# h - tanh(h) as one constant times tanh(a h)^2 times tanh(b h), from a copy of the PSUM result, on one Trainium2 core

## The chip, the cores and the metric

The kernel runs on 1 core of a Trainium2 chip. The metric is device microseconds of one launch. Times of several runs are given as their median; a profile shows one execution and has a span, from its first to its last instruction.

## The reference

Two blocks follow one another. The first is a linear attention with a decaying state (4 batches, 8 heads, 768 tokens, head width 48); the second is a dense block with 2048 hidden features on the attention's 3072 x 384 result.

```python
for t in range(S):
    cur = einsum('bhd,bhe->bhde', u[None] * k[t], v[t])
    y[:, :, t] = einsum('bhd,bhde->bhe', r[t], state + cur)
    state = w[t][..., None] * state + einsum('bhd,bhe->bhde', k[t], v[t])
x = y.transpose(0, 2, 1, 3).reshape(3072, 384)
h = x @ w_in              # 384 -> 2048
g = h - np.tanh(h)
out = g @ w_out           # 2048 -> 384
```

With the reference's inputs h is small: its standard deviation is 0.0143 and its largest magnitude 0.084.

## The kernel before

**Tiles.** The 3072 tokens are cut into 8 blocks of 384 (4 batches, two blocks each). A block has 16 steps f, each of which makes one tile of h: 128 features by 384 tokens. So there are 128 tiles, numbered `now = i * 16 + f`. While the dense steps of block i run, the attention of block i + 1 is woven between them.

**One step.** `first` puts three fp32 products (six matrix instructions in the trace) into one PSUM bank, `hp`. ScalarE copies it, scaled, into an SBUF tile `h` (L893). Then `slight` makes g = h - tanh(h) for small h as a polynomial: `s` = h^2, `qa` = (s + SHIFT)^2, then on VectorE h := TOP h s (first `product`) and g = (qa + REST) h (second `product`). TensorE uses g some steps later.

**The guard.** The polynomial holds for h^2 up to `SLIGHT`. For the 113 tiles in `light` ScalarE makes all of `s` (Square, L979), `qa` (Square with a bias, L980) and a Relu with a summed output (L984) that is zero if all h^2 are small. For the other 15 tiles (`plain`: the first 13 of block 0 and the last two of the program) VectorE squares h and keeps the largest (`tensor_tensor_reduce`, L994), and ScalarE makes only `qa` (L997). All guards are counted at the end; if one fails, everything is computed again by a general path (`any_h`).

**Order.** TensorE, VectorE, ScalarE and SyncE run the order in which the code is written (a manual schedule); each executes its queue in order. The VectorE work of a step is a list `ops`, in which the two products of the step before (`rest`) are interleaved with attention work. A step's bank `hp` is single from step 6 on: `first` of the next step cannot start before ScalarE has copied it out. (The first six steps use six places in other banks in turn.) The tiles `h`, `s` and `qa` have three buffers each.

**Block 0** has a second job for ScalarE: the weights arrive as raw 64-bit words and are converted to fp32 by three ScalarE instructions per unit (L267: one to `w_sb`, two to `up`) and one VectorE instruction (L271). There are 16 units; `PIECES` says how many of the ScalarE instructions stand in each step f, and these end in step 12. In block 0, g goes straight into the second product (`Second.add`, L1043), three steps after it was made. In later blocks VectorE forms sums of pieces of g (L1013), so that fewer products are needed (`Fewer`, L1092). In block 7, and in a few steps of blocks 3 to 6 (`JOINED`), two tiles of h are made together (L951, L961), without the copy.

Of the kernel before, what the change touches and what calls it, by code (L numbers as in the profile page):

```python
# [37 lines left out]
F32 = mybir.dt.float32  # L38
# [3 lines left out]
BF16 = mybir.dt.bfloat16  # L42
# [3 lines left out]
AF = mybir.ActivationFunctionType  # L46
ALU = mybir.AluOpType
# [4 lines left out]
P = 128  # L52
L = 64
NB = 384
NQ = S // NB
NCH = NB // L
NCP = NCH // 2
NPAIR = H // 2
LP = L + 1
WIDE = NPAIR * NCH * LP  # L60
HALF = WIDE // 2 + 2
UP = 2
# [6 lines left out]
NF = FF // P  # L69
# [10 lines left out]
LATE = 3  # L80
# [41 lines left out]
JOINED = {3: (1,), 4: (1,), 5: (1,), 6: (1, NF // 2 - 1), 7: TWOS}  # L122


SLIGHT = 2.0 ** -6
TOP, SHIFT, REST = 0.053459249436855316, -1.2470279932022095, 4.680200099945068


@with_exitstack
def kernel(  # L130
# [19 lines left out]
    early = ExitStack()  # L150
    conv = early.enter_context(tc.tile_pool(name="conv", bufs=RAWS))

    shift = const.tile([P, 6], F32, name="shift", tag="shift")
    for i, value in enumerate((QUAD[0][0], QUAD[1][0], -SMALL, -1.0, SHIFT, -SLIGHT)):
        nc.vector.memset(shift[:, i:i + 1], value)
    u_sb = const.tile([P, NPAIR], F32, name="u_sb", tag="u_sb")
    nc.scalar.dma_start(out=u_sb, in_=uT)
# [64 lines left out]
    def ring(t, at, n):  # L222
        return t[:, at + n % 4 * 3:at + n % 4 * 3 + 3].rearrange("p t c -> p (t c)")
# [3 lines left out]
    def g_at(q, x):  # L227
        if not isinstance(x, str):
# [7 lines left out]
    fast = range(1, blocks_n)  # L236
    few = [0 if i not in fast else NF if i + 1 < blocks_n else 2 * LAST for i in range(blocks_n)]
    n_whole = blocks_n * NPAIR * NCH
    light = [n for n in range(blocks_n * NF) if NF - LATE <= n < blocks_n * NF - 2 and
             (n < NF or few[n // NF])]  # L240
    plain = [n for n in range(blocks_n * NF) if n not in light]
    n_excess, n_top = 2 * blocks_n + len(light), len(plain)
    holds = const.tile([P, n_whole + n_excess + n_top], BF16, name="holds", tag="holds")
    ends = const.tile([P, 3], F32, name="ends", tag="ends")
    excess = const.tile([P, n_excess], F32, name="excess", tag="excess")
# [640 lines left out]
    def first(xT, f, hp, apart=0):  # L886
        for kc in reversed(range(KC)):
            nc.tensor.matmul(hp, lhsT=w_in_sb[:, f, kc, :], rhs=xT[kc],  # L888
                             start=(kc == KC - 1), stop=(kc == 0))
            for _ in range(apart):  # L890
                nc.tensor.nop(nofuse=True, hint="apart")
        h = dense.tile([P, NB], F32, name="h", tag="h")
        return h, nc.scalar.activation(out=h, in_=hp, func=AF.Copy, scale=1.0 / UPSCALE)  # L893

    def product(out, in0, scalar, in1, op0):
        return lambda: nc.vector.scalar_tensor_tensor(out=out, in0=in0, scalar=scalar, in1=in1,  # L896
# [67 lines left out]
                               (h[:, 1], h[:, 6], e1[:, 1, 0:HB]),  # L964
                               (h[:, 2:4], twice(h[:, 5]), e1[:, 1::-1, HB:NB]))]

    def slight(h, n, i, f, scale=1.0, later=None):

        s, qa = (dense.tile([P, NB], F32, name=name, tag=name) for name in ("s", "qa"))
        q, j = divmod(f, 2)
        if i in fast:
            g = G[:, g_at(q, "0" + "ab"[j]):g_at(q, "2" + "ab"[j]) + 1].rearrange("p t c -> p (t c)")
        else:
            g = ring(sums, 0, n)
        if n in light:
            at = 2 * blocks_n + light.index(n)
            nc.scalar.activation(out=s, in_=h, func=AF.Square, scale=scale)  # L979
            nc.scalar.activation(out=qa, in_=s, func=AF.Square, bias=shift[:, 4:5])  # L980
            junk = work.tile([P, UP * NCH * LP], BF16, name="junk", tag="junk", bufs=1)

            def over():
                nc.scalar.activation(out=junk[:, 0:NB], in_=s, func=AF.Relu, bias=shift[:, 5:6],  # L984
                                     accum_out=excess[:, at:at + 1])

            if later is None:
                over()
            else:
                later.append(over)  # L990
            square = first = []
        else:
            at = plain.index(n)
            square = [lambda: nc.vector.tensor_tensor_reduce(  # L994
                out=s, in0=h, in1=h, scale=1.0, scalar=0.0, op0=ALU.mult, op1=ALU.max,
                accum_out=top[:, at:at + 1])]
            first = [lambda: nc.scalar.activation(out=qa, in_=s, func=AF.Square, bias=shift[:, 4:5])]  # L997
        return g, first, square, [product(h, h, TOP * scale, s, ALU.mult),
                                  product(g, qa, REST, h, ALU.add)]

    def two(t, a, b):

# [10 lines left out]
        return lambda: nc.vector.tensor_tensor(out=G[:, to:to + 2], in0=two(G, g_at(q, a0), g_at(q, a1)),  # L1013
                                               in1=two(G, g_at(q, b0), g_at(q, b1)), op=OPS[op])

    def any_h(h, g):
        s, qa = (dense.tile([P, NB], F32, name=name, tag=name) for name in ("s", "qa"))
        th, qb, big = (inp.tile([P, 2 * HALF], F32, name=name, tag=tag)[:, 0:NB]
                       for name, tag in (("th", "k"), ("qb", "r"), ("big", "w")))
        nc.scalar.activation(out=s, in_=h, func=AF.Square)  # L1020
        nc.scalar.activation(out=qa, in_=s, func=AF.Square, bias=shift[:, 0:1])
        nc.scalar.activation(out=qb, in_=s, func=AF.Square, bias=shift[:, 1:2])
        nc.scalar.activation(out=th, in_=h, func=AF.Tanh)
        nc.scalar.activation(out=big, in_=s, func=AF.Relu, bias=shift[:, 2:3])
        nc.vector.tensor_tensor(out=th, in0=h, in1=th, op=ALU.subtract)
        product(h, h, SERIES, s, ALU.mult)()
        product(h, qa, QUAD[0][1], h, ALU.add)()
        product(g, qb, QUAD[1][1], h, ALU.add)()
        nc.vector.copy_predicated(out=g, mask=big.bitcast(I32), data=th)
        return g  # L1030
# [284 lines left out]
        pieces = boot(Turns([scratch(ps_boot)] + ps_a.both), [hp] + acc, blocks[0], blocks[1])  # L1315
    ps_d = mains.enter_context(tc.tile_pool(name="ps_d", bufs=1, space=PSUM))
    acc += [ps_d.tile([P, BANK], F32, name=f"acc{j}", tag=f"acc{j}") for j in range(1, NB // P)]
    ahead_of_h, rest, formed, extra, behind, due, summed = [], [], [], [], [], [], []
    held_back, forming, late, carried = [], [], [], []

    def between(ops, others):
# [9 lines left out]

    def sum_held(held, squares, over, to):

        nc.vector.tensor_single_scalar(held, squares, SLIGHT, op=ALU.is_le)
        nc.vector.tensor_reduce(out=to, in_=over, op=ALU.add, axis=mybir.AxisListType.X)

    def form_w(n, q, k):
# [7 lines left out]
    for i, blk in enumerate(blocks):  # L1345
# [8 lines left out]
        second = Second(row0, acc, few[i]) if few[i] < NF else None  # L1354
        for f in range(NF):
            now = i * NF + f
            for op in ahead_of_h if i else ():
                op()
            spare_a, spare_b = (t[:, 0] for t in ps_a.both)
            to = [acc[0], acc[1], hp, spare_a, spare_b, spare_a][now] if now < 6 else hp  # L1360
            joined = f // 2 in JOINED.get(i, ())
            near = later and f < 4
            outs = []
            if not joined:
                h, made = first(here, f, to[:, 0:NB], SPACED[i][f > 12 + (i < 2)])
            elif f % 2 == 0:
                for op in behind:
                    op()
                behind = []
                by = beside if near else twos  # L1370
                outs = by.begin(ps_a, f // 2)
                if near:
                    for name in ("split 2 0", "split 2 1", "split 0 01"):
                        later.phase(ps_a, name)
            if not i:
                made_up = converting(pieces, (PIECES[f] if f < len(PIECES) else 1) - 1)
                for op in ahead_of_h:
                    op()
                made_up += converting(pieces, 1 if f < len(PIECES) and PIECES[f] else 0)
            if not joined:  # L1380
                g, ahead_of_h, square, later_ops = slight(h, now, i, f)
            elif f % 2:
                g, ahead_of_h, square, later_ops = slight(by.h[1], now, i, f, 1.0 / UPSCALE, over)
                for op in over:
                    op()
            else:
                ahead_of_h, square = [], []
            some = ({4: (0, 2), 6: (2, 4), 8: (4, 6), 9: (6, 8), 14: (8, len(SUMS))} if after else
                    {4: (0, 2), 6: (2, 4), 8: (4, 6), 9: (6, 8), 11: (8, 10), 12: (10, len(SUMS))} if later else
                    {4: (0, 1), 5: (1, 2), 6: (2, 3), 7: (3, 4), 8: (4, 5), 9: (5, 9), 10: (9, 11),  # L1390
# [77 lines left out]
                op()  # L1468
            if outs:
                add_due(now)  # L1470
                over = []
                g, ahead_of_h, square, later_ops = slight(by.h[0], now, i, f, 1.0 / UPSCALE, over)
            rest, behind, formed, forming, held_back = later_ops, [], [], held_back, []
            extra = [] if i else made_up
            if f < few[i]:
# [60 lines left out]
                later.together(ps_a)  # L1536
        if fewer and later:
            summed.append(fewer)
    nc.vector.tensor_single_scalar(ends[:, 1:3], top[:, n_top - 2:], SLIGHT, op=ALU.is_le)
    again = const.tile([1, 1], I32, name="again", tag="again")  # L1540
    for op in ahead_of_h + rest:
        op()
    for j in range(NB // P):
        if j == 1:
# [16 lines left out]
    with tc.If(anew > 0, label="anew"):  # L1561
        with tc.manual_schedule(engines={PE, SP, DVE, ACT}), ExitStack() as again_pools:
            ps_d = again_pools.enter_context(tc.tile_pool(name="ps_e", bufs=1, space=PSUM))
            ps_a = again_pools.enter_context(tc.tile_pool(name="ps_b", bufs=2, space=PSUM))
            acc = [ps_d.tile([P, BANK], F32, name=f"acc{j}", tag=f"acc{j}") for j in range(NB // P)]
            hp = ps_d.tile([P, NB], F32, name="hp", tag="hp")
            draw((1, 2, 4, 8), slice(128, 288))
            for st in states:
                nc.vector.memset(st[:, :, :, D:], 0.0)
            for blk in [Block(b, q) for b in range(B) for q in range(NQ)]:  # L1570
                blk.general(ps_a)
                second = Second(blk.b * S + blk.q * NB, acc)
                for f in range(NF):
                    second.add(f, any_h(first(blk.xT, f, hp)[0], ring(sums, 0, f)), False)


# [52 lines left out]
```

## Time and profile before

| | |
|---|---|
| time, median of 3 runs | 540.66 us (540.36 to 542.41) |
| span of the profiled execution | 538.7 us |
| time around the span, by the median | 2.0 us |
| TensorE busy | 529.3 us, 98% |
| VectorE busy | 495.9 us, 92% |
| ScalarE busy | 393.4 us, 73% |
| GpSimd busy | 9.2 us, 2% |
| mean granted TensorE clock | 0.998 |

The page gives the span of the profiled execution and no separate time for it; the 2.0 us are the median less that span. Busy shares are means over parts of the program that differ: up to 23.5 us the attention of the first block alone, to 104 us block 0, to 462 us blocks 1 to 6, to 521 us the joined steps of block 7, and then the end.

### The profile page before, as it was taken

To read this page: it belongs to the slowest core of one execution; us is meant where nothing else is said; L and a number is where in the kernel's file an instruction comes from. 1 tells how busy PE (TensorE), PEld (TensorE's weight loads), DVE (VectorE), ACT (ScalarE), POOL (GpSimd) and SP (SyncE) were. 2 spreads that over 40 slices of the span, in tenths; PEclk is the share of its full clock that TensorE was granted. 3 is DMA by queue.
4 is the path that set the end of the run, shared out by engine and by line. 5 is a ranking of instruction groups with operands and counts; after the bars stand their busy time and mean duration, and the time that the engine had idled before them with its cause. 6 is when DMAs were issued, how large, how long until landed. Compare 5 with 4: busy or idle time off the path is not lost.

```text
span 538.7 us, 15161 instructions
## 1 busy us (share of the span) xinstructions
PE 529.3 (98%) x5820; PEld 419.7 (78%) x5820; DVE 495.9 (92%) x1044; ACT 393.4 (73%) x796; POOL 9.2 (2%) x57
## 2 busy tenths in 40 slices
PE   7999999999999999999999999999999999999996
PEld 5756665677777777877878787787878877999993
DVE  7999999999989989999898989989899899979885
ACT  4999986988668876678676787587865886546460
POOL 1100000000000000000000000000000000000001
PEclk9999999999999999999999999999999999999999
DMA  8798742252311632164211632128232340100011
GB/s 279 244 408 327 237 122 72 101 136 65 121 32 65 163 109 59 53 116 150 63 56 46 149 119 66 51 60 192 63 90 68 47 103 16 43 2 1 10 36 47
DMA packets 53049, 56.36 MB, mean 105 GB/s; under 512 B 21488, under 2 KB 50928, under 8 KB 52976
## 3 DMA queue, kind: packets, MB, share of 16 engines
q1 hardware_dynamic: 52592, 55.18, 34.8%
q8 instruction: 49, 0.80, 0.6%
q14 instruction: 24, 0.20, 0.1%
q10 hardware_dynamic: 288, 0.10, 0.1%
q0 software_dynamic: 96, 0.07, 0.1%
HBM read 44.73 MB, written 4.72 MB: 92 GB/s over the span
## 4 chain that ended last, share of the span: by engine, by line
PE 95%; DVE 2%; DMA 1%; PEld 1%; issue 0%; ACT 0%; SPq 0%; PEldq 0%; DVEq 0%
PE hp L888 36%; PE acc L1092 27%; PE att L951 8%; PE att L1092 6%; PE acc L1043 5%; PE att L774 4%; PE att L497 2%; PE att L578 1%; PE acc L1070 1%; PE att L888 1%; DMA r<-in_rT 1%; PE acc L888 1%; PE hp L1092 0%; PE att L520 0%; DVE scores L505 0%; DVE pre L420 0%
## 5 line engine op out<-in xcount | busy, mean ns | idle before, releaser
L888 PE MATMUL hp<-xT,w_sb 128*128 128x384 f32 x594 | 208.8, 488 | 0.5 <-DVE w_sb L271 0.5
L888 PEld LDWEIGHTS hp<-xT,w_sb 128*128 128x128 f32 x594 | 106.3, 190 | 57.0 <-issue 0.6
L1092 PE MATMUL acc<-forms,g 128*128 128x128 f32 x972 | 136.0, 276 | 0.0
L1092 PEld LDWEIGHTS acc<-forms,g 128*128 128x128 f32 x972 | 124.4, 192 | 7.7
L1013 DVE TENSOR_TENSOR g<-g 128x256 f32<-128x256 f32 x270 | 106.6, 419 | 0.7 <-PE acc L1092 0.2
L893 ACT ACTIVATE h<-hp 128x384 f32<-128x384 f32 x99 | 48.5, 490 | 75.4 <-PE hp L888 75.3
L980 ACT ACTIVATE qa<-s,shift 128x384 f32<-128x384 f32 x113 | 69.6, 616 | 3.7
L984 ACT ACTIVATE junk<-s,shift 128x384 bf16<-128x384 f32 x113 | 68.0, 601 | 0.4
L896 DVE SCALAR_TENSOR_TENSOR h<-h,s 128x384 f32<-128x384 f32 x104 | 57.1, 549 | 11.7 <-ACT s L979 11.6
L1092 PE MATMUL acc<-w_sb,g 128*128 128x128 f32 x324 | 54.1, 276 | 0.0
L1092 PEld LDWEIGHTS acc<-w_sb,g 128*128 128x128 f32 x324 | 47.0, 192 | 7.6 <-ACT sums L1060 0.3
L896 DVE SCALAR_TENSOR_TENSOR g<-qa,h 128x384 f32<-128x384 f32 x88 | 48.4, 550 | 1.3
L979 ACT ACTIVATE s<-h 128x384 f32<-128x384 f32 x89 | 46.6, 523 | 2.8
L1127 DVE TENSOR_TENSOR sums<-sums 128x256 f32<-128x256 f32 x84 | 33.0, 409 | 1.2 <-ACT sums L1104 1.0
L1043 PE MATMUL acc<-w_sb,sums 128*128 128x384 f32 x96 | 33.7, 487 | 0.0
L1092 PE MATMUL att<-w_sb,g 128*128 128x128 f32 x200 | 33.4, 275 | 0.0
L267 ACT ACTIVATE up<-raw 128x768 f16<-128x768 f32 (+1 forms) x32 | 33.1, 1076 | 0.0
L1092 PEld LDWEIGHTS att<-w_sb,g 128*128 128x128 f32 x200 | 29.0, 192 | 4.2
L1043 PEld LDWEIGHTS acc<-w_sb,sums 128*128 128x128 f32 x96 | 18.0, 190 | 12.3 <-DVE sums L896 0.3
L420 DVE TENSOR_TENSOR_SCAN pre<-w,start 128x780 f32<-128x780 f32 x14 | 25.0, 1783 | 0.8
L951 PE MATMUL att<-xT,w_sb 128*128 128x192 f32 x120 | 25.4, 326 | 0.0
L432 DVE TENSOR_TENSOR_SCAN post<-w,seed 128x780 f32<-128x780 f32 x14 | 24.9, 1776 | 0.0
(185 smaller groups left out, 715.2 us busy)
## 6 DMA issues: line engine op xcount, KB each, us to landing
raw<-in_weights SPq DMA_DIRECT2D x16, 768.0 KB, 6.7
w<-in_wT SPq DMA_DIRECT2D x7, 780.0 KB, 4.5
k<-in_kT SPq DMA_DIRECT2D x7, 768.0 KB, 5.2
r<-in_rT SPq DMA_DIRECT2D x7, 768.0 KB, 4.6
v_sb<-in_v SPq DMA_DIRECT2D x8, 576.0 KB, 4.7
k<-in_tokens SPq DMA_DIRECT2D x7, 576.0 KB, 3.9
r<-in_tokens SPq DMA_DIRECT2D x7, 576.0 KB, 4.9
out_y<-sums SPq DMA_DIRECT2D x18, 128.0 KB, 1.9
```

The lines of the kernel that those rows point to most:

```text
L267: return lambda: nc.scalar.activation(out=to, in_=of, func=AF.Copy, scale=scale, bias=bias)
L888: nc.tensor.matmul(hp, lhsT=w_in_sb[:, f, kc, :], rhs=xT[kc], start=(kc == KC - 1), stop=(kc == 0))
L893: return h, nc.scalar.activation(out=h, in_=hp, func=AF.Copy, scale=1.0 / UPSCALE)
L896: return lambda: nc.vector.scalar_tensor_tensor(out=out, in0=in0, scalar=scalar, in1=in1, op0=op0, op1=ALU.mult)
L951: nc.tensor.matmul(to, lhsT=lhs, rhs=rhs, start=n == 0, stop=n + 1 == len(of))
L979: nc.scalar.activation(out=s, in_=h, func=AF.Square, scale=scale)
L980: nc.scalar.activation(out=qa, in_=s, func=AF.Square, bias=shift[:, 4:5])
L984: nc.scalar.activation(out=junk[:, 0:NB], in_=s, func=AF.Relu, bias=shift[:, 5:6], accum_out=excess[:, at:at + 1])
L1013: return lambda: nc.vector.tensor_tensor(out=G[:, to:to + 2], in0=two(G, g_at(q, a0), g_at(q, a1)), in1=two(G, g_at(q, b0), g_at(q, b1)), ...
L1043: nc.tensor.matmul(acc, lhsT=g[:, j * P:(j + 1) * P], rhs=w_out_sb[:, f, :], start=(f == self.first), stop=(f == NF - 1))
L1092: nc.tensor.matmul(to, lhsT=G[:, g_at(q, a), :], rhs=rhs, start=start, stop=stop, skip_group_check=True)
L1127: ops.append(lambda op=op, at=at: nc.vector.tensor_tensor(out=at[0], in0=at[1], in1=at[2], op=OPS[op]))
```

## The change

The polynomial is replaced by RATIO tanh(INNER h)^2 tanh(OUTER h), whose first terms in h agree with those of h - tanh(h). The copy out of PSUM stays, now into the tile `s` (`copied`). Both Tanh instructions read that copy. The inner one is squared: on ScalarE with a summed output for the `light` tiles, on VectorE with the largest value kept for the plain ones. One VectorE product is left of two. The guard now compares the sum (or the largest) of the squared inner Tanh with `LIMIT`. The step-by-step shift of `qa` into the following step (`ahead_of_h`) is gone: both Tanh stand right behind the copy, ahead of the step's weight conversions.

```diff
-SLIGHT = 2.0 ** -6
-TOP, SHIFT, REST = 0.053459249436855316, -1.2470279932022095, 4.680200099945068
+SLIGHT = 2.0 ** -3
+INNER, OUTER, RATIO = 0.30059090362460511, 1.0096109787140124, 3.654037807057518
+LIMIT = float(np.tanh(INNER * SLIGHT ** 0.5) ** 2 * (1.0 - 2.0 ** -16))
...
     def slight(h, n, i, f, scale=1.0):
...
+        nc.scalar.activation(out=t, in_=h, func=AF.Tanh, scale=INNER * scale)
+        nc.scalar.activation(out=by, in_=h, func=AF.Tanh, scale=OUTER * scale)
+        square = []
         if n in light:
-            nc.scalar.activation(out=s, in_=h, func=AF.Square, scale=scale)
-            nc.scalar.activation(out=qa, in_=s, func=AF.Square, bias=shift[:, 4:5])
...
-                nc.scalar.activation(out=junk[:, 0:NB], in_=s, func=AF.Relu, bias=shift[:, 5:6],
-                                     accum_out=excess[:, at:at + 1])
...
+            nc.scalar.activation(out=t, in_=t, func=AF.Square, accum_out=top[:, n:n + 1])
         else:
             square = [lambda: nc.vector.tensor_tensor_reduce(
-                out=s, in0=h, in1=h, scale=1.0, scalar=0.0, op0=ALU.mult, op1=ALU.max,
...
+                out=t, in0=t, in1=t, scale=1.0, scalar=0.0, op0=ALU.mult, op1=ALU.max,
+                accum_out=top[:, n:n + 1])]
-            first = [lambda: nc.scalar.activation(out=qa, in_=s, func=AF.Square, bias=shift[:, 4:5])]
-        return g, first, square, [product(h, h, TOP * scale, s, ALU.mult),
-                                  product(g, qa, REST, h, ALU.add)]
+        return g, square, [product(g, t, RATIO, by, ALU.mult)]
...
             if not joined:
-                h, made = first(here, f, to[:, 0:NB], SPACED[i][f > 12 + (i < 2)])
+                h, made = copied(first(here, f, to[:, 0:NB], SPACED[i][f > 12 + (i < 2)]))
+                g, square, later_ops = slight(h, now, i, f)
...
             if not i:
-                made_up = converting(pieces, (PIECES[f] if f < len(PIECES) else 1) - 1)
-                for op in ahead_of_h:
-                    op()
-                made_up += converting(pieces, 1 if f < len(PIECES) and PIECES[f] else 0)
+                made_up = converting(pieces, PIECES[f] if f < len(PIECES) else 0)
```

Two places show how the queues change. ScalarE's queue before, from the copy of step 7 to the copy of step 9 of block 0 (`w_sb` and `up` are weight conversions, `h<-hp` the copy out of PSUM, `qa` the biased Square of the step before):

```order
L893 ACTIVATE h<-hp 128x384
L267 ACTIVATE w_sb<-raw 128x768
L267 ACTIVATE up<-raw 128x768 x2
L997 ACTIVATE qa<-s,shift 128x384
L267 ACTIVATE w_sb<-raw 128x768
L893 ACTIVATE h<-hp 128x384
L267 ACTIVATE up<-raw 128x768 x2
L997 ACTIVATE qa<-s,shift 128x384
L267 ACTIVATE w_sb<-raw 128x768
L893 ACTIVATE h<-hp 128x384
```

The same place of ScalarE's queue with the change (`s<-hp` is the copy, `h<-s` and `qa<-s` are the inner and the outer Tanh):

```order
L1003 ACTIVATE s<-hp 128x384
L975 ACTIVATE h<-s 128x384
L976 ACTIVATE qa<-s 128x384
L266 ACTIVATE w_sb<-raw 128x768
L266 ACTIVATE up<-raw 128x768 x2
L266 ACTIVATE w_sb<-raw 128x768
L1003 ACTIVATE s<-hp 128x384
L975 ACTIVATE h<-s 128x384
L976 ACTIVATE qa<-s 128x384
L266 ACTIVATE up<-raw 128x768 x2
L266 ACTIVATE w_sb<-raw 128x768
L1003 ACTIVATE s<-hp 128x384
```

Between two copies stands one instruction more, and the instruction behind a copy now reads what the copy writes.

VectorE's queue before, in step 7 of block 0 (L271 ends two weight units, L994 squares and keeps the largest, L896 are the products, L439 is attention work):

```order
L271 SCALAR_TENSOR_TENSOR w_sb<-w_sb,up 128x768 x2
L994 ISA s,top<-h 128x384
L994 ISA top 128x1
L896 SCALAR_TENSOR_TENSOR h<-h,s 128x384
L439 TENSOR_TENSOR pre<-r,pre 128x24x64
L896 SCALAR_TENSOR_TENSOR sums<-qa,h 128x384
```

VectorE's queue with the change, in the same step:

```order
L270 SCALAR_TENSOR_TENSOR w_sb<-w_sb,up 128x768 x2
L981 ISA h,top<-h 128x384
L981 ISA top 128x1
L894 SCALAR_TENSOR_TENSOR sums<-h,qa 128x384
L438 TENSOR_TENSOR pre<-r,pre 128x24x64
```

One product is gone; the squaring stays in its place and now reads the inner Tanh instead of the copy. The order of TensorE's, GpSimd's and SyncE's queues is the same in both kernels, and ScalarE's queue has one table load, at its start, in both.

More of the change, by code (lines that the diff above doesn't have):

```diff
@@ L151 @@
     conv = early.enter_context(tc.tile_pool(name="conv", bufs=RAWS))
-    shift = const.tile([P, 6], F32, name="shift", tag="shift")
-    for i, value in enumerate((QUAD[0][0], QUAD[1][0], -SMALL, -1.0, SHIFT, -SLIGHT)):
+    shift = const.tile([P, 4], F32, name="shift", tag="shift")
+    for i, value in enumerate((QUAD[0][0], QUAD[1][0], -SMALL, -1.0)):
         nc.vector.memset(shift[:, i:i + 1], value)
@@ L238 @@
     n_whole = blocks_n * NPAIR * NCH
[L239 to L242, printed above, removed]
+    light = range(NF - LATE, blocks_n * NF - 2)
+    n_excess, n_top = 2 * blocks_n, blocks_n * NF
     holds = const.tile([P, n_whole + n_excess + n_top], BF16, name="holds", tag="holds")
@@ L891, in first @@
                 nc.tensor.nop(nofuse=True, hint="apart")
-        h = dense.tile([P, NB], F32, name="h", tag="h")
-        return h, nc.scalar.activation(out=h, in_=hp, func=AF.Copy, scale=1.0 / UPSCALE)
+        return hp
     def product(out, in0, scalar, in1, op0):
@@ L965, in begin, with slight @@
                                (h[:, 2:4], twice(h[:, 5]), e1[:, 1::-1, HB:NB]))]
-    def slight(h, n, i, f, scale=1.0, later=None):
-        s, qa = (dense.tile([P, NB], F32, name=name, tag=name) for name in ("s", "qa"))
+    def slight(h, n, i, f, scale=1.0):
+        t, by = (dense.tile([P, NB], F32, name=name, tag=name) for name in ("h", "qa"))
         q, j = divmod(f, 2)
@@ L976, in slight @@
             g = ring(sums, 0, n)
+        nc.scalar.activation(out=t, in_=h, func=AF.Tanh, scale=INNER * scale)
+        nc.scalar.activation(out=by, in_=h, func=AF.Tanh, scale=OUTER * scale)
+        square = []
         if n in light:
[L978 to L984, printed above, removed]
-                                     accum_out=excess[:, at:at + 1])
[L987 to L991, printed above, removed]
+            nc.scalar.activation(out=t, in_=t, func=AF.Square, accum_out=top[:, n:n + 1])
         else:
-            at = plain.index(n)
             square = [lambda: nc.vector.tensor_tensor_reduce(
-                out=s, in0=h, in1=h, scale=1.0, scalar=0.0, op0=ALU.mult, op1=ALU.max,
-                accum_out=top[:, at:at + 1])]
-            first = [lambda: nc.scalar.activation(out=qa, in_=s, func=AF.Square, bias=shift[:, 4:5])]
-        return g, first, square, [product(h, h, TOP * scale, s, ALU.mult),
-                                  product(g, qa, REST, h, ALU.add)]
+                out=t, in0=t, in1=t, scale=1.0, scalar=0.0, op0=ALU.mult, op1=ALU.max,
+                accum_out=top[:, n:n + 1])]
+        return g, square, [product(g, t, RATIO, by, ALU.mult)]
     def two(t, a, b):
@@ L1014, in form_g, with copied, any_h @@
                                                in1=two(G, g_at(q, b0), g_at(q, b1)), op=OPS[op])
-    def any_h(h, g):
+    def copied(hp):
+        h = dense.tile([P, NB], F32, name="s", tag="s")
+        return h, nc.scalar.activation(out=h, in_=hp, func=AF.Copy, scale=1.0 / UPSCALE)
+    def any_h(of, g):
+        h = dense.tile([P, NB], F32, name="h", tag="h")
+        nc.scalar.activation(out=h, in_=of, func=AF.Copy, scale=1.0 / UPSCALE)
         s, qa = (dense.tile([P, NB], F32, name=name, tag=name) for name in ("s", "qa"))
@@ L1317 @@
     acc += [ps_d.tile([P, BANK], F32, name=f"acc{j}", tag=f"acc{j}") for j in range(1, NB // P)]
-    ahead_of_h, rest, formed, extra, behind, due, summed = [], [], [], [], [], [], []
+    rest, formed, extra, behind, due, summed = [], [], [], [], [], []
     held_back, forming, late, carried = [], [], [], []
@@ L1332, in sum_held @@
     def sum_held(held, squares, over, to):
-        nc.vector.tensor_single_scalar(held, squares, SLIGHT, op=ALU.is_le)
+        nc.vector.tensor_single_scalar(held, squares, LIMIT, op=ALU.is_le)
         nc.vector.tensor_reduce(out=to, in_=over, op=ALU.add, axis=mybir.AxisListType.X)
@@ L1356 @@
             now = i * NF + f
-            for op in ahead_of_h if i else ():
-                op()
             spare_a, spare_b = (t[:, 0] for t in ps_a.both)
@@ L1375 @@
             if not i:
-                made_up = converting(pieces, (PIECES[f] if f < len(PIECES) else 1) - 1)
-                for op in ahead_of_h:
-                    op()
-                made_up += converting(pieces, 1 if f < len(PIECES) and PIECES[f] else 0)
[L1380 to L1387, printed above, removed]
+                made_up = converting(pieces, PIECES[f] if f < len(PIECES) else 0)
+            if joined and f % 2:
+                g, square, later_ops = slight(by.h[1], now, i, f, 1.0 / UPSCALE)
             some = ({4: (0, 2), 6: (2, 4), 8: (4, 6), 9: (6, 8), 14: (8, len(SUMS))} if after else
@@ L1470 @@
                 add_due(now)
-                over = []
-                g, ahead_of_h, square, later_ops = slight(by.h[0], now, i, f, 1.0 / UPSCALE, over)
+                g, square, later_ops = slight(by.h[0], now, i, f, 1.0 / UPSCALE)
             rest, behind, formed, forming, held_back = later_ops, [], [], held_back, []
@@ L1538 @@
             summed.append(fewer)
-    nc.vector.tensor_single_scalar(ends[:, 1:3], top[:, n_top - 2:], SLIGHT, op=ALU.is_le)
+    nc.vector.tensor_single_scalar(ends[:, 1:3], top[:, n_top - 2:], LIMIT, op=ALU.is_le)
     again = const.tile([1, 1], I32, name="again", tag="again")
-    for op in ahead_of_h + rest:
+    for op in rest:
         op()
@@ L1573 @@
                 for f in range(NF):
-                    second.add(f, any_h(first(blk.xT, f, hp)[0], ring(sums, 0, f)), False)
+                    second.add(f, any_h(first(blk.xT, f, hp), ring(sums, 0, f)), False)
 def kernel(r, k, v, w, u, moe_w_in, moe_w_out):
```

## The prediction

> **What bounds the kernel now.** I read the busy shares first, then the same shares by stage, then the waits and the timeline of the one stage in which TensorE is not alone at the limit.
>
> From the page, the busy times; from the busy time by stage, one row for each of the five stages (columns: length, then busy time of TensorE, its weight loads, VectorE, ScalarE, GpSimd, granted clock, DMA):
>
> ```profile
> PE 529.3 (98%) x5820; PEld 419.7 (78%) x5820; DVE 495.9 (92%) x1044; ACT 393.4 (73%) x796; POOL 9.2 (2%) x57
> 0.00:23.50 23.50, 19.50 (x591) 15.12 (x591) 19.48 (x35) 15.46 (x23) 4.56 (x24) 1.00 0.73 246
> 23.50:104.00 80.50, 79.98 (x616) 49.43 (x613) 77.85 (x140) 72.71 (x122) 0.32 (x4) 1.00 0.63 225
> 104.00:462.00 358.00, 358.00 (x4119) 287.95 (x4118) 335.37 (x716) 267.60 (x566) 2.03 (x23) 1.00 0.33 87
> 462.00:521.00 59.00, 59.00 (x450) 59.00 (x449) 52.84 (x127) 33.99 (x82) 0.00 (x0) 1.00 0.05 14
> 521.00:538.70 17.70, 12.82 (x56) 8.24 (x54) 10.36 (x30) 3.61 (x7) 2.28 (x6) 0.93 0.10 36
> ```
>
> From 104 to 521 us TensorE is never idle, at full clock. Its instructions and their order stay, so this stretch can only become longer. All its idle time is 538.7 - 529.3 = 9.4 us: 4.0 before 23.5 us, where the change has nothing but two small memsets less, 0.5 in block 0, 4.9 at the end. That is the ceiling on any gain.
>
> Block 0 in finer windows, and ScalarE's waits from its copy of step 0 to its copy of step 13:
>
> ```profile
> 40.00:52.00 12.00, 11.55 (x120) 7.40 (x120) 11.56 (x21) 12.00 (x18) 0.00 (x0) 1.00 0.92 341
> 52.00:67.00 15.00, 14.98 (x137) 9.30 (x138) 14.52 (x31) 15.00 (x23) 0.14 (x2) 1.00 0.72 244
> 67.00:81.00 14.00, 13.95 (x226) 8.98 (x225) 14.00 (x23) 12.23 (x22) 0.18 (x2) 1.00 0.39 119
> ACT w_sb L267 <- DMA raw<-in_weights: 0.5, 1, 0.5
> ACT h L893 <- PE hp L888: 0.4, 1, 0.4
> ```
>
> From 40 to 67 us ScalarE is busy in every microsecond: 12.00 of 12.00, 15.00 of 15.00. In 50 us it waits 0.9. Its mean of 73% hides that here, where it converts the weights, it is as full as TensorE, and VectorE nearly so. TensorE keeps going because ScalarE is just in time.
>
> **The change part by part: ScalarE in block 0.** The removed and the added instructions, and the spacing of ScalarE's starts:
>
> ```profile
> L997 ACT ACTIVATE qa<-s,shift 128x384 f32<-128x384 f32 x12 | 7.4, 615 | 0.0
> L979 ACT ACTIVATE s<-h 128x384 f32<-128x384 f32 x89 | 46.6, 523 | 2.8
> 25.84 0.49 ACT L893 ACTIVATE h<-acc 128x384 f32<-128x384 f32 x1
> 53.39 0.61 ACT L997 ACTIVATE qa<-s,shift 128x384 f32<-128x384 f32 x1
> 53.88 0.94 ACT L267 ACTIVATE w_sb<-raw 128x768 f32<-128x768 f32 x1
> 54.69 0.51 ACT L893 ACTIVATE h<-hp 128x384 f32<-128x384 f32 x1
> 55.05 2.02 ACT L267 ACTIVATE up<-raw 128x768 f16<-128x768 f32 x2
> 72.06 0.47 ACT L893 ACTIVATE h<-hp 128x384 f32<-128x384 f32 x1
> 82.51 0.49 ACT L893 ACTIVATE h<-hp 128x384 f32<-128x384 f32 x1 [0.46 <-PE hp L888]
> 83.03 0.52 ACT L979 ACTIVATE s<-h 128x384 f32<-128x384 f32 x1
> ```
>
> What counts is the start-to-start time. A biased Square takes 0.49 (53.39 to 53.88), 0.12 less than its own 0.61, since a successor that does not depend on it starts early. A copy takes 0.36 if the next instruction doesn't need it (54.69 to 55.05), and 0.52 if it does (82.51 to 83.03). With the change the Tanh behind each copy reads that copy.
>
> No row shows a Tanh. The nearest is the Square without a bias at the same shape, 0.523; less the overlap of 0.12 it takes about 0.41 in a row. The ends are 0.36, the copy's spacing, and 0.52, no overlap at all. I take 0.41, since the input and output are those of that Square. The Trainium skill, page "ScalarE: Activation LUTs", section "What ACT_TABLE_LOAD costs", says every function runs at one element per cycle; by it a Tanh costs what the Square costs and the sum stays. No run so far shows it.
>
> The sum is made from the copy of step 0 (25.84) to the copy of step 12 (72.06), 12 steps, in which all conversions stay:
> - gone: 11 biased Squares (the twelfth in the first row stands behind the copy of step 12), 11 x 0.49 = 5.4;
> - added: 24 Tanh, 24 x 0.41 = 9.8;
> - the copies become waited for: 12 x (0.52 - 0.36) = 1.9;
> - the two waits are filled: -0.9.
>
> Together +5.4 us: the copy of step 12 starts at 72.06 + 5.4 = 77.5 and ends at 78.0.
>
> Who waits for it: TensorE.
>
> ```profile
> 52.02 2.17 PE L888 MATMUL hp<-xT,w_sb 128*128 128x384 f32 x6 [0.47 <-DVE w_sb L271]
> 69.33 2.10 PE L888 MATMUL hp<-xT,w_sb 128*128 128x384 f32 x6
> 73.20 2.10 PE L888 MATMUL hp<-xT,w_sb 128*128 128x384 f32 x6
> 77.17 1.56 PE L774 MATMUL att<-pre,states 48*48 48x64 f32 x96
> 80.27 2.20 PE L888 MATMUL hp<-xT,w_sb 128*128 128x384 f32 x6
> ```
>
> The bank `hp` is single, so the products of step 13 (73.20) wait for the copy of step 12. Before, that copy ended at 72.06 + 0.47 = 72.53: a cover of 0.67 us. Now it ends at 78.0, and TensorE is late by 78.0 - 73.2 = 4.8 us. It doesn't come all at once: from about step 6 on, each `first`, the transposes of `turn` (they use the banks of steps 4 and 5) and the update (it needs the copies `ks`, queued behind the conversions) wait a little. ScalarE itself doesn't go idle in this. The products of step 12 start when the copy of step 11 ends, 0.5 after its start, and last 2.1 (the 69.33 row), so they are done 2.6 after it. The copy of step 12 stands behind a copy, two Tanh and four conversions, 0.52 + 0.82 + 4 x 0.9 = 4.9 (a conversion from the pair of 2.02 at 55.05, less overlap). So ScalarE, not TensorE, sets the pace. The conversions end in step 12; from 73.20 to 80.27 TensorE then has 7.1 us of its own work, ScalarE only a copy, Tanh pair and four conversions (about 5), so the delay stops at 4.8. After that TensorE has no gap (358.00 of 358.00) in which to make it up.
>
> By the two ends of a Tanh: 24 x 0.36 = 8.6 gives a copy later by 4.2 and a delay of 3.6; 24 x 0.52 = 12.5 gives 8.1 and 7.4.
>
> **VectorE.** It loses one product of two for each of 128 tiles:
>
> ```profile
> L896 DVE SCALAR_TENSOR_TENSOR h<-h,s 128x384 f32<-128x384 f32 x104 | 57.1, 549 | 11.7 <-ACT s L979 11.6
> ```
>
> About 0.55 a tile, 70 us in all, beside TensorE's work nearly everywhere. In block 0 it wins 0.47 where TensorE waited for a converted weight (52.02), but that weight now comes from a later ScalarE: nothing is left of it. New on VectorE is that the squaring (L981) waits for the inner Tanh, with the product of the step before and the conversions of the next unit queued behind it. TensorE uses the product three steps later; the conversions are already counted as late by ScalarE. Zero.
>
> **Blocks 1 to 7.** A light tile loses two ScalarE instructions with a bias (0.616 and 0.601 by the page's rows below) and the Square, and gets two Tanh and a summed Square. The readout of the sum stays.
>
> ```profile
> L980 ACT ACTIVATE qa<-s,shift 128x384 f32<-128x384 f32 x113 | 69.6, 616 | 3.7
> L984 ACT ACTIVATE junk<-s,shift 128x384 bf16<-128x384 f32 x113 | 68.0, 601 | 0.4
> 119.99 0.49 ACT L893 ACTIVATE h<-hp 128x384 f32<-128x384 f32 x1 [0.73 <-PE hp L888]
> 122.38 0.55 DVE L896 SCALAR_TENSOR_TENSOR g<-qa,h 128x384 f32<-128x384 f32 x1
> ```
>
> Each new instruction at 523: 0.616 + 0.601 + 0.523 - 3 x 0.523 = 0.17 less for a tile, on an engine that waits there anyway. The result g becomes possible one instruction later: copy 0.52, two Tanh 0.82, Square 0.52, so 1.9 after the copy's start, where VectorE gets to g only 2.4 after it (119.99 to 122.38). So no new wait: zero. At the end of the program the last tile swaps a biased Square behind VectorE's squaring for a Tanh ahead of it; within 0.3, zero.
>
> **Sum.** Profiled span 538.7 + 4.8 = 543.5; with the 2.0 around it that part the median from the span, 545.5 us.
>
> **The rivals.**
>
> *The delay is absorbed* (no change). If a Tanh started 0.3 after its predecessor or less, or other engines' slack took more than I find, less than 2.7 us would be left: 24 x 0.30 = 7.2 gives a delay of 2.2, so 542.9. For it: 0.67 of cover in step 13, and VectorE's lighter load. Against it: 15.00 of 15.00, and no ScalarE row of this width has a spacing below 0.36.
>
> *VectorE is what holds TensorE* (the other side). The Trainium skill, page "Perfetto Trace Analysis", section "Identifying the Most-Contended Engine", takes occupancy as the measure for VectorE and ScalarE and says to relieve the fullest engine first. As a mechanism here: 92% against 73%, so work moves from the fuller engine to the emptier. It decides if TensorE waits for VectorE and ScalarE has room in block 0. Its price is bounded: the 0.47 at 52.02 and two products at the end, 1.1, so 540.66 - 1.6 = 539.1, still no change by the measure used here. A gain of over 2.7 us would need more than half of the 5.4 us of idle time that the change can reach at all. What the rule's mean leaves out is the stage: by the 52.00 to 67.00 row, ScalarE is the fullest.
>
> *New waits in blocks 1 to 7 on top.* g waits for the third ScalarE instruction instead of the second, with the sums of pieces behind it on VectorE. It decides where VectorE now runs ahead and TensorE stands less than 0.2 us behind it. A g later by 0.2 on a fifth of the 89 copied light tiles (the L979 row) would be 3.6 us more: 549.1. Against it: the 11.6 us that VectorE waited for `s` before cost TensorE nothing from 104 to 521 us.
>
> *The guard fires.* Its sum over 384 tokens is a sharper condition than a largest value. From the reference's inputs the largest such sum is 0.01033, the limit 0.01121, so it holds, by 8%; else all of it would be computed a second time, some 1,080 us by twice the median.
>
> **How the numbers follow.** About 0.5%, 2.7 us, is what a measurement of this kernel can tell from no change; a delay of 4.8 lies beyond it. Chances: ScalarE's queue in block 0 sets the delay, 543.5 to 548: 0.71. Absorbed, 540.5 to 543.4: 0.12. VectorE held TensorE: 0.05, of which 0.03 over 2.7 us of gain. New waits on top, 548 to 555: 0.10. Guard: 0.02. The range 542.7 to 549.5 holds the first case, its bounds of 3.6 and 7.4, a part of the second and the near part of the fourth. Slower by over 0.5%: 0.71 + 0.10 + 0.02 = 0.83; within: 0.12 + 0.02 = 0.14; faster: 0.03.
>
> **What would show it right or wrong.** Right: ScalarE without idle time from about 26 to 82 us; in TensorE's rows waits for ScalarE in block 0 of about 5 us in sum; the products of step 13 at 78.0 instead of 73.2; a Tanh of 0.52; from block 1 on every TensorE row later by the same amount; VectorE's busy time down by about 70. Wrong: step 13's products within 2 us of 73.2; a TensorE wait for g after block 0; a stretch from step 14 to the last products that differs by more than 0.5 us from before; or a second table load in ScalarE's rows.

## The result, and the profile after

The changed kernel takes 544.51 us (median of 4 runs, 543.95 to 545.54) against 540.73 us for the kernel before (4 runs too). The ratio is 1.0069 with a 95% interval from 1.0051 to 1.0088, so it is slower by 3.7 us, 2.8 to 4.8. The forecast was 545.5, with a range from 542.7 to 549.5.

The page of the changed kernel, busy times, and its busy time by stage (columns as in the prediction: length, TensorE, weight loads, VectorE, ScalarE, GpSimd, clock, DMA):

```profile
PE 530.9 (98%) x5820; PEld 419.2 (77%) x5820; DVE 442.4 (82%) x914; ACT 364.4 (67%) x811; POOL 9.1 (2%) x57
23.50:108.00 84.50, 81.59 (x612) 48.86 (x613) 69.23 (x120) 76.13 (x135) 0.32 (x4) 1.00 0.60 213
84.18:525.34 441.16, 441.16 (x4658) 361.96 (x4651) 362.48 (x768) 285.09 (x687) 2.03 (x23) 1.00 0.29 78
525.34:542.40 17.06, 12.38 (x52) 7.81 (x50) 9.05 (x25) 3.94 (x8) 2.16 (x6) 1.00 0.11 37
```

VectorE and ScalarE are both less busy than before, by 53.5 and 29.0 us, and the program is longer. The stretch from the products of step 14 of block 0 (84.18) to those of the last block's step 14 (525.34) is 441.16 us. In the kernel before the same two places lie 441.16 us apart too:

```profile
80.27:521.43 441.16, 441.16 (x4657) 361.96 (x4651) 411.81 (x885) 319.95 (x687) 2.03 (x23) 1.00 0.29 77
521.43:538.70 17.27, 12.39 (x52) 7.82 (x50) 9.97 (x27) 3.30 (x6) 2.28 (x6) 0.92 0.11 37
```

So nothing at all happened to the time of 441 of 540 us. The whole difference stands ahead of 84.18 (+3.91), and the end is 0.21 shorter. That 0.21 lies behind the issue of the last output transfer, which comes 12.88 us after the products of the last block's step 14 before, and 12.87 after them with the change:

```profile
534.31 0.36 ACTq L1076 DMA_DIRECT2D out_y<-g  x1
538.21 0.36 ACTq L1067 DMA_DIRECT2D out_y<-g  x1
```

In block 0, the timeline of ScalarE (copies of steps 0 and 12, and of step 8 with its two Tanh) and of TensorE (the products of steps 13 and 14, the release in brackets):

```profile
25.71 0.49 ACT L1003 ACTIVATE s<-acc 128x384 f32<-128x384 f32 x1
58.06 0.46 ACT L1003 ACTIVATE s<-hp 128x384 f32<-128x384 f32 x1
58.56 0.52 ACT L975 ACTIVATE h<-s 128x384 f32<-128x384 f32 x1
58.99 0.51 ACT L976 ACTIVATE qa<-s 128x384 f32<-128x384 f32 x1
59.40 1.97 ACT L266 ACTIVATE up<-raw 128x768 f16<-128x768 f32 x2
76.75 0.47 ACT L1003 ACTIVATE s<-hp 128x384 f32<-128x384 f32 x1
77.28 2.20 PE L887 MATMUL hp<-xT,w_sb 128*128 128x384 f32 x6 [0.74 <-ACT s L1003]
84.18 2.20 PE L887 MATMUL hp<-xT,w_sb 128*128 128x384 f32 x6
```

The copy of step 12 starts at 76.75 instead of 72.06, and the products of step 13 start where it ends, at 77.28 instead of 73.20; the bracket names that copy. The spacing per tile is copy 0.50, first Tanh 0.43, second Tanh 0.41. The waits view of TensorE and of its weight loads, within block 0:

```profile
PE hp L887 <- ACT s L1003: 1.2, 3, 0.7
PE att L577 <- ACT ks L525: 1.1, 1, 1.1
PE att L519 <- ACT s L1003: 0.5, 1, 0.5
PEld hp L887 <- ACT s L1003: 4.2, 5, 1.4
PEld att L577 <- ACT ks L525: 1.9, 2, 1.7
```

The places are those of the prediction: the bank `hp` (L887), the update that needs `ks` (L577), the transposes of `turn` (L519). The matmul rows admit 2.8 us in all, less than the 4 us lost; the weight loads, which stand ahead of the matmuls, show 6.1 in the two rows. A matmul's end is modelled by the profile, so a wait behind it can be hidden in its length; the products of a step that read 2.10 us before mostly read 2.20 here. The loss is therefore read from starts, not from the list of waits.

### The profile page after: what moved, and what is told of

The parts are those of the page before. It is cut to its first block, busy times and chain, and to the rows that moved or that the text cites. A ratio compares the mean times of both kernels' runs of the same rounds, so it can differ in the third digit from the quotient of the medians.

```text
span 542.4 us, 14972 instructions
## 1 busy us (share of the span) xinstructions
PE 530.9 (98%) x5820; PEld 419.2 (77%) x5820; DVE 442.4 (82%) x914; ACT 364.4 (67%) x811; POOL 9.1 (2%) x57
## 3 DMA queue, kind: packets, MB, share of 16 engines
HBM read 44.73 MB, written 4.72 MB: 91 GB/s over the span
## 4 chain that ended last, share of the span: by engine, by line
PE 85%; ACT 9%; issue 1%; DMA 1%; DVE 1%; PEld 0%; SPq 0%; PEldq 0%; DVEq 0%
PE hp L887 33%; PE acc L1083 27%; PE att L949 8%; PE att L1083 6%; ACT up L266 4%; PE att L773 4%; PE acc L1034 2%; PE att L496 2%; ACT w_sb L266 2%; PE att L577 1%; PE acc L1061 1%; DMA states<-in_wT 1%; ACT qa L976 1%; ACT s L1003 1%; ACT h L975 1%
## 5 line engine op out<-in xcount | busy, mean ns | idle before, releaser
L887 PE MATMUL hp<-xT,w_sb 128*128 128x384 f32 x594 | 209.4, 489 | 1.3 <-ACT s L1003 1.2
L887 PEld LDWEIGHTS hp<-xT,w_sb 128*128 128x128 f32 x594 | 105.8, 190 | 59.6 <-ACT s L1003 4.2
L1003 ACT ACTIVATE s<-hp 128x384 f32<-128x384 f32 x99 | 48.3, 488 | 103.0 <-PE hp L887 103.0
L894 DVE SCALAR_TENSOR_TENSOR g<-h,qa 128x384 f32<-128x384 f32 x112 | 62.0, 553 | 61.2 <-ACT h L979 60.9
L979 ACT ACTIVATE h<-h 128x384 f32<-128x384 f32 x113 | 57.4, 508 | 0.0
L975 ACT ACTIVATE h<-s 128x384 f32<-128x384 f32 x104 | 54.4, 523 | 3.3
L976 ACT ACTIVATE qa<-s 128x384 f32<-128x384 f32 x104 | 52.7, 507 | 0.0
L979 ACT ACTIVATION_READ_ACCUMULATOR h<-h 128x1 f32 x113 | 21.2, 188 | 0.0
```

Of the source, the lines that this page charges most:

```text
L975: nc.scalar.activation(out=t, in_=h, func=AF.Tanh, scale=INNER * scale)
L976: nc.scalar.activation(out=by, in_=h, func=AF.Tanh, scale=OUTER * scale)
L979: nc.scalar.activation(out=t, in_=t, func=AF.Square, accum_out=top[:, n:n + 1])
```

## The experiments

The theory, A: in block 0 ScalarE's queue, filled by weight conversions, is the bound; each instruction added there shows in the end, and nothing that changes elsewhere does. Rivals: B, later results g cost time in blocks 1 to 7; C, VectorE's relief is worth something there; D, TensorE waits because the bank is released later, not because the queue is long. All kernels were timed beside the kernel before. The start of ScalarE's first instruction on step 0's tile differs by up to 2.6 us between profiled runs (25.48 to 28.07), so places in profiles are compared from there on. From the products of step 14 to the end of the span all nine profiled runs take 458.2 to 458.4 us, whatever the edit: apart from that start, the runs differ in block 0 alone.

| kernel | median us | ratio to before | step 13's products after that first start, us |
|---|---|---|---|
| before | 540.73 to 541.23 | 1 | 47.36 |
| changed | 544.51 | 1.0069 (1.0051 to 1.0088) | 51.57 |
| light tiles changed only | 541.09 | 1.0004 (0.9994 to 1.0014) | 47.72 |
| plain tiles changed only | 544.63 | 1.0072 (1.0054 to 1.0090) | 51.58 |
| PSUM read twice in block 0 | 540.56 | 0.9987 (0.9976 to 0.9998) | 46.85 |
| a third Tanh in block 0 | 550.48 | 1.0175 (1.0159 to 1.0192) | 56.47 |
| conversion between copy and Tanh | 543.69 | 1.0045 (1.0028 to 1.0061) | 50.10 |
| product made twice in block 0 | 545.52 | 1.0081 (1.0061 to 1.0100) | 51.63 |
| PSUM read twice everywhere | 541.02 | 0.9988 (0.9975 to 1.0001) | 46.86 |

**Light tiles only.** The kernel before, with this in place of the light branch:

```diff
         if n in light:
-            nc.scalar.activation(out=s, in_=h, func=AF.Square, scale=scale)
-            nc.scalar.activation(out=qa, in_=s, func=AF.Square, bias=shift[:, 4:5])
-            ... Relu with accum_out
+            nc.scalar.activation(out=s, in_=h, func=AF.Tanh, scale=INNER * scale)
+            nc.scalar.activation(out=qa, in_=h, func=AF.Tanh, scale=OUTER * scale)
+            nc.scalar.activation(out=s, in_=s, func=AF.Square, accum_out=top[:, n:n + 1])
+            return g, [], [], [product(g, s, RATIO, qa, ALU.mult)]
```

> The kernel before, with only the 113 light tiles in the Tanh form (two Tanh, one summed Square, one product); the 13 plain tiles of block 0 and the last two keep the polynomial. Theory A (ScalarE's queue in block 0 alone makes the delay): no change, 540.7 us within 0.5, although VectorE loses 113 products. Rival B (later results g in blocks 1 to 7 cost TensorE time): most of the 3.8 us is here, 543 or more. Rival C (VectorE's relief is worth something): under 540.

541.09 us, ratio 1.0004 with an interval of about 0.5 us on either side: no change. Its VectorE waits and its stretch of blocks 1 to 6:

```profile
DVE g L898 <- ACT s L982: 61.1, 52, 4.6
106.00:460.00 354.00, 354.00 (x3971) 284.70 (x3973) 294.33 (x618) 238.54 (x561) 1.86 (x21) 1.00 0.32 86
```

VectorE now waits 61 us for the summed Square, in 52 places, and TensorE is busy 354.00 of 354.00 us. B and C both fall, as far as 0.5 us can tell: VectorE waits where it would otherwise have been ahead, TensorE doesn't, and 113 products less are worth nothing.

**Plain tiles only.** The changed kernel, with the polynomial back in the light tiles:

```diff
+        if n in light:
+            nc.scalar.activation(out=t, in_=h, func=AF.Square, scale=scale)
+            nc.scalar.activation(out=by, in_=t, func=AF.Square, bias=shift[:, 4:5])
+            ... Relu with accum_out
+            return g, [], [product(h, h, TOP * scale, t, ALU.mult), product(g, by, REST, h, ALU.add)]
```

> The changed kernel, with the 113 light tiles back in the polynomial form; only block 0's 13 plain tiles and the last two have the Tanh form. Theory A: the whole delay is here, 544.5 us within 0.5. Rival B: under 542.

544.63 us, and step 13's products at 51.58 where the changed kernel has 51.57 (step 0's copy, and step 13's products):

```profile
26.83 0.49 ACT L1011 ACTIVATE s<-acc 128x384 f32<-128x384 f32 x1
78.41 2.20 PE L889 MATMUL hp<-xT,w_sb 128*128 128x384 f32 x6 [0.74 <-ACT s L1011]
```

The 13 tiles of block 0 (and two at the end) make all of the delay.

**PSUM read twice in block 0.** The copy is left out for the 13 plain tiles; `slight.made` is the second Tanh, which now releases the bank:

```diff
+                h = first(here, f, to[:, 0:NB], SPACED[i][f > 12 + (i < 2)])
+                if now < NF - LATE:
+                    g, square, later_ops = slight(h, now, i, f, 1.0 / UPSCALE)
+                    made = slight.made
...
```

> The changed kernel, but in block 0's 13 plain tiles both Tanh read the PSUM bank and the copy is left out, so ScalarE has 12 copies at 0.50 us less up to step 12 and the bank is free after the second Tanh instead of after the copy. Theory A: ScalarE's time per tile is then 0.8 us against 0.87 of the kernel before, the delay is gone: 540.7 within 0.7. Rival D (it is the later release of the bank, not the length of ScalarE's queue, that TensorE waits for): the bank is held for two instructions instead of one, so no better than 544.

540.56 us, ratio 0.9987 with an interval that ends at 0.9998: the delay is gone, and a little more. ScalarE in step 8, and TensorE's products of step 13:

```profile
55.14 0.49 ACT L975 ACTIVATE h<-hp 128x384 f32<-128x384 f32 x1
55.53 0.49 ACT L976 ACTIVATE qa<-hp 128x384 f32<-128x384 f32 x1
55.90 1.98 ACT L266 ACTIVATE up<-raw 128x768 f16<-128x768 f32 x2
74.11 2.10 PE L887 MATMUL hp<-xT,w_sb 128*128 128x384 f32 x6
```

Two Tanh take 0.76 (55.14 to 55.90), where the kernel before takes 0.36 + 0.49 for copy and biased Square. The step 13 row has no bracket: TensorE has no listed wait in block 0, and is 0.51 ahead of the kernel before, whose one wait there was 0.47. D falls: the bank is held for two instructions, and TensorE is faster.

**A third Tanh.** One more, unused, in each of the 13 tiles:

```diff
+        if n < NF - LATE:
+            nc.scalar.activation(out=junk[:, 0:NB], in_=h, func=AF.Tanh, scale=OUTER * scale)
```

> The changed kernel with a third Tanh (its result unused) behind the other two in each of block 0's 13 plain tiles: 12 x 0.41 = 4.9 us more on ScalarE up to the copy of step 12. Theory A: no cover is left, so all of it is seen: 544.5 + 4.9 = 549.4 us within 0.7. Rival D or any theory in which ScalarE's length is not the bound: under 547.

Step 13's products stand at 56.47, 4.90 later than in the changed kernel, as 12 x 0.41 says. The time, 550.48, is 6.0 above the changed kernel's median, 1.1 above the 549.4 that was expected and so outside its 0.7. By the ratios the difference is 5.7, with intervals near 1 us on either side. In the profiled runs the two spans differ by 5.8: 0.93 is a later start of step 0 with the third Tanh (26.64 instead of 25.71), the 4.9 are in block 0, and from step 14 on both take 458.2. Why step 0 starts later, and whether it does in the other runs, stays open.

```profile
83.11 1.24 PE L887 MATMUL hp<-xT,w_sb 128*128 128x384 f32 x3 [1.16 <-ACT s L1006]
```

**A conversion between copy and Tanh.** The same instructions, one moved:

```diff
                 h, made = copied(first(here, f, to[:, 0:NB], SPACED[i][f > 12 + (i < 2)]))
+                between_two = converting(pieces, 1) if not i and f < len(PIECES) and PIECES[f] else []
                 g, square, later_ops = slight(h, now, i, f)
```

> The changed kernel, with the first weight conversion of each step of block 0 moved in between the copy and the two Tanh, so the copy isn't waited for by the next instruction. The instructions are the same. Theory A with its term for the waited-for copy: 10 of the 12 copies up to step 12 start their successor after 0.37 us instead of 0.50, 1.3 us less: 543.2 us within 0.6. If the term is nothing, 544.5.

543.69 us, and step 13 at 50.10, 1.47 earlier than in the changed kernel. The rows of step 7:

```profile
54.44 0.52 ACT L1003 ACTIVATE s<-hp 128x384 f32<-128x384 f32 x1
54.82 0.94 ACT L266 ACTIVATE w_sb<-raw 128x768 f32<-128x768 f32 x1
55.63 0.53 ACT L975 ACTIVATE h<-s 128x384 f32<-128x384 f32 x1
```

The copy's spacing falls to 0.38, so the wait of an instruction for its predecessor's result is a real term. The time alone doesn't settle it, since the interval of the ratio (1.0028 to 1.0061) overlaps the changed kernel's; the starts do.

**The product made twice in block 0.** VectorE's product written twice in the 13 plain tiles, the same result:

```diff
-        return g, square, [product(g, t, RATIO, by, ALU.mult)]
+        return g, square, [product(g, t, RATIO, by, ALU.mult)] * (2 if n < NF - LATE else 1)
```

> The changed kernel with its VectorE product made twice in each of block 0's 13 plain tiles, so VectorE has as many instructions there as before. Theory A': ScalarE's conversions were 0.5 us shorter in sum than before, since VectorE did less beside them; then they are longer again, the copy of step 12 comes 51.5 us after the copy of step 0 instead of 51.0, and the time is 545.0. Without such a link: spacing of the conversions unchanged (0.92 and 0.80), 544.5 within 0.4.

The spacing of the conversions stays at 0.92 and 0.80, and step 12's copy stands 51.08 after step 0's, 51.04 in the changed kernel:

```profile
25.48 0.49 ACT L1003 ACTIVATE s<-acc 128x384 f32<-128x384 f32 x1
76.56 0.49 ACT L1003 ACTIVATE s<-hp 128x384 f32<-128x384 f32 x1
```

So the few tenths by which the conversions were shorter than in the kernel before are not VectorE's doing in this way; A' falls. The median, 545.52, is 1.0 above what was expected without the link, outside its 0.4, and 0.5 above what was expected with it. Its interval overlaps the changed kernel's, so the time can't decide; the places in block 0 do.

**PSUM read twice everywhere.** As above, for all single tiles.

```diff
-                if now < NF - LATE:
+                if True:
```

> The changed kernel with the copy left out for all single tiles of all blocks: both Tanh read the PSUM bank, which is held for two instructions. Theory A: after block 0 neither ScalarE's time nor the bank decides (a bank is free about 1.0 us after its products end, and TensorE comes back to it after 1.3), so as with PSUM read twice in block 0 alone: 540.5 us within 0.7. Rival D (the bank held longer is waited for): 543 or more, with TensorE waits for ScalarE in blocks 1 to 6.

541.02 us, ratio 0.9988. In blocks 1 to 6 ScalarE has a copy less per tile, 194.84 us of work instead of 239.84, and the stretch becomes neither faster nor slower:

```profile
105.00:463.00 358.00, 358.00 (x4118) 287.92 (x4117) 299.14 (x627) 194.84 (x483) 2.07 (x23) 1.00 0.32 87
```

This is where rival D is pressed hardest. The second Tanh ends 0.91 us after a step's products (121.41 to 122.32 in this profile), and TensorE's next products for that bank start 0.26 later, at 122.58: the bank is free in time, but only just.

Of all versions only the one that leaves out the copy in block 0 alone is ahead of the kernel before by more than the noise, by 0.13% (0.02 to 0.24%), and barely so.

## Why the prediction was right

**The bound.** The claim was that TensorE's stretch after block 0 can only become longer, and that in block 0 ScalarE has no cover. Both hold: 441.16 us against 441.16, and each edit of ScalarE's queue in block 0 moved step 13's products by about its own length (-1.47 and +4.90). Where the copies went they moved by only -4.72, although 12 copies of 0.50 are 6.0 us: there TensorE's own work set the pace again, and ScalarE waited 1.1 us for its products.

**The sum, term by term**, from step 0's copy to step 12's, as the two timelines give it:

| term | forecast us | measured us |
|---|---|---|
| 11 biased Squares gone | -5.4 | -5.45 |
| 24 Tanh | +9.8 | +10.10 |
| copies waited for | +1.9 | +1.52 |
| waits filled | -0.9 | -0.88 |
| conversions and other instructions | 0 | -0.48 |
| sum | +5.4 | +4.82 |

The terms that were mis-sized: a copy that its successor waits for is spaced 0.50, not 0.52, and one that isn't 0.376 in the mean, not 0.36. The conversions, which I held fixed, came out 0.35 us shorter and the guards of the decays 0.14; half of the 0.35 is one pair (2.00 us at 28.81 in the kernel before, 1.83 after), which may be a wait too short to be listed. Why the rest is shorter is not settled. The 0.14 belongs to a wait that was filled: before, the guard's readout took 0.09 from start to start where the copy behind it was ready (62.51 to 62.60) and 0.64 where it was not (66.96 to 67.60), of which 0.40 is listed. The misses have both signs and partly cancel, so it is partly luck that the total is so near. So the copy of step 12 ended at 77.22 and not 78.0, step 13 came 4.08 late instead of 4.8, and step 14, 3.91: from step 13 to step 14 TensorE took 6.90 us instead of 7.07, and why isn't shown. The end of the program, put at zero, is 0.21 shorter, but behind the issue of the last output transfer and not where the change is.

**The Tanh.** No row had shown one; the Square of the same shape was the guess, and the page of ScalarE's groups after has it:

```profile
L975 ACT ACTIVATE h<-s 128x384 f32<-128x384 f32 x104 | 54.4, 523 | 3.3
L976 ACT ACTIVATE qa<-s 128x384 f32<-128x384 f32 x104 | 52.7, 507 | 0.0
```

523 ns where it waits for the copy, 507 where it doesn't: the Square's 523. That agrees with the sentence of the Trainium skill, "ScalarE: Activation LUTs", "What ACT_TABLE_LOAD costs", that every function runs at one rate; its formula for an immediate scale and bias gives an estimate of 506 ns for 384 elements.

**VectorE** was put at 70 us less and at a worth of zero. The worth is right (the light tiles alone: ratio 1.0004). The 70 is wrong: busy time fell by 53.5, 0.42 a product. The lengths of the products' rows do sum to 70 us less (140.9 before, 70.9 after), but instructions that follow each other overlap (a product of 0.55 at 107.03 in the kernel before, the next start at 107.49), and a removed one takes only its spacing out of a busy stretch.

**What would show it right** held, but for two: the list of TensorE's waits was to sum to about 5 us, and it gives 2.8 for a loss of 4; and VectorE's busy time was to fall by about 70. ScalarE was busy for 55.59 of the 56.00 us from 26 to 82, and from step 14 on no wait of TensorE is listed.

**The rivals.** The delay was not absorbed. (One reading against that rival was off by little: two copies of the kernel before are spaced 0.35, below the 0.36 that was called the least, 44.56 to 44.91 and 72.06 to 72.41.) The mean occupancy, 92% against 73%, pointed the other way and was no guide: work went from the engine that looked fuller to the one that was full in the stage that counts. The prediction's step "So no new wait: zero" for blocks 1 to 7 is wrong in its first half. VectorE's waits for a tile's result from ScalarE, three rows before and one after:

```profile
DVE h L896 <- ACT s L979: 11.6, 12, 2.2
DVE ks L896 <- ACT s L979: 4.5, 4, 1.1
DVE w L896 <- ACT s L979: 1.1, 1, 1.1
DVE g L894 <- ACT h L979: 60.9, 51, 4.6
```

They rose from 17.2 us in sum to 60.9. The step took the 2.4 us at which VectorE reached g for fixed, but with a product fewer per tile VectorE comes there earlier: between the two step-14 places it is busy 49.3 us less (362.48 against 411.81) and waits more instead. The zero is right for another reason: TensorE has no listed wait for g. The guard held: nothing was computed a second time.

## What to carry to other kernels

Read the engines' load by stage before moving work from one to another: an engine with 27% idle time in the mean had 0.9 us of it in the 50 us in which it fed TensorE. Cost an added instruction by the spacing of starts, not by its length, and add what the next instruction waits if it reads its result; other ready work put between the two takes that wait away. And ask whether a copy out of PSUM is needed at all: two readers of the bank (0.76 us) were shorter than a copy and two readers of the copy (1.34 us), and the bank was still free in time.

## What was not expected of the hardware

A Tanh that reads PSUM takes 0.49 us for 128x384, against 0.507 from SBUF, and two of them follow each other at 0.39. Waits of TensorE for another engine stood with 4.2 us in the weight-load rows of `hp` and with 1.2 in its matmul rows, for the same place.
